# Another order of evictions, maxima and scaling between the batches of an attention block, and contiguous one-hots in the routing behind it

## The chip, the cores and the metric

The kernel runs on one core of a Trainium2 chip. Its engines work through queues of their own, each in its own order: TensorE (PE; its weight loads are shown as PEld), VectorE (DVE), ScalarE (ACT), GpSimd (POOL), and SyncE (SP), which issues most of the transfers. The metric is the device time of one execution in microseconds (us), the median of several runs.

## What is computed

An attention between tokens and states in 8 batches and 8 heads, whose output, 8 x 544 rows of 512 numbers, goes through a mixture of 8 experts:

```python
B, H, S, Ns, D = (8, 8, 512, 32, 64)
scores = scale * np.matmul(x, state.transpose(0, 1, 3, 2))
a = np.exp(scores - scores.max(-1, keepdims=True))
a /= a.sum(-1, keepdims=True) + 1e-09
xread = np.matmul(a, state)                     # tokens read states
scores2 = scale * np.matmul(state, x.transpose(0, 1, 3, 2))
a2 = np.exp(scores2 - scores2.max(-1, keepdims=True))
a2 /= a2.sum(-1, keepdims=True) + 1e-09
sread = np.matmul(a2, x)                        # states read tokens
...                                             # concat of both, heads side by side: x (8, 544, 512)
logits = x @ w_gate
local_gate = sigmoid(x @ w_local)
e = argmax(logits) if s == 0 or local_gate < 0.5 else the expert of the token before
out = softmax(logits)[e] * (np.maximum(x @ w1[e], 0.0) @ w2[e])
```

## The kernel before

The program has three stages: attention, batch by batch; routing, which decides the expert of every row and sorts the rows into blocks of 128 slots with one expert each; and the experts, block by block (38 blocks with this input). Nothing schedules the instructions: every engine takes them in the order in which the code is written.

**Attention.** `Attention.run` works on two batches at once: while `now` reads, `then`, the next batch, gets its weights. The methods of `Batch`:

- `scores` (L254, PE) forms states x tokens for all heads in two PSUM banks, `s0` and `s1`. Each has only one buffer.
- `over_tokens` takes, for each bank, the maximum over the tokens on DVE (L264, L265: `nb`) and the exponential with its sum on ACT (L268: `e2`, `z2`); DVE also writes the scores transposed in blocks of 32 into `e1` (L273).
- `over_states` takes the reciprocal of `z2` and the maximum over the states (L286, `m1`) on DVE and subtracts it on POOL (L287). `exponents` (L291, ACT) is the exponential of that, `shares` the sums and their reciprocal on DVE (L300 to L302) and the division on POOL (L303).
- `scale` (L295, ACT) multiplies `e2` by the reciprocals. `turn` (L315) transposes it on PE into the banks `t0` and `t1`, and ACT copies it out to `e` (L316). `turn_back` (L307, DVE) transposes `e1` back to `a`.
- `state_reads` multiplies `e` by the tokens on PE (L325, in bank `t0`), copies on ACT (L330, `rt`), transposes on DVE (L333, `ys`) and stores the rows through SP (L335).
- `token_reads(c)` multiplies a quarter of `a` by the states on PE (L343), in two alternating PSUM buffers `v`, and copies the result to `xr` (L346): on ACT for c = 0 and 2, on DVE for c = 1 and 3.
- `logits` multiplies `rt` by the gate's weights on PE (L352, in bank `t1`), adds up the token logits on POOL (L355), copies the states' logits to `lt` on DVE (L356), and stores `xr` (L358). The next batch's second group of transposes uses bank `t1` again.

`load_t` and `load_n` issue a batch's `x_t` (L169, two transfers) and `x_n` (L175, one) on SP, two batches ahead. `gates` fills the last columns of `sd`, which the token reads multiply by (L191 on PE, L195 on ACT). `Routing.constants` and `more_constants` write small constants (L395 to L421 on DVE); `place` (L388, ACT) holds, for every k, the number k repeated over the 40 columns.

**Routing** is mostly one chain of DVE instructions on 128 x 40 rows. `keep(n)` puts n products on PE that nobody reads (L433, bank `idle`). The chain gives every row a slot, split into block (`blk`) and place in it (`pos`). `inb` says which block a row is in, `inp` which place (both one-hot), and `slotted` (L554) multiplies them over the 40 columns, once for the rows' numbers (`who`, from `bc`) and once for their probabilities (from `pb`). `slots.row` (L576) tells POOL which rows to gather (L613); the gathered rows are transposed on DVE (L618, `xt`) for the first products of the experts (L642). Their weights `a` and `c`, 4 MB a block, come through SP (L627).

Of the kernel before, what the change touches and what calls it, by code (L numbers as in the profile page):

```python
# [10 lines left out]
BF16 = mybir.dt.bfloat16  # L11
Act = mybir.ActivationFunctionType
Alu = mybir.AluOpType
# [5 lines left out]
P = 128  # L19
B, H, S, N, DH = 8, 8, 512, 32, 64  # L20
# [4 lines left out]
SC = S // P  # L25
# [96 lines left out]
class Attention:  # L122


    def __init__(self, ctx, tc, xn, xt, st, stt, wgl, wgs, lt, rows):
# [16 lines left out]
        x_t = self.load_t(0)  # L142
        nc.sync.dma_start(out=self.sttc[1], in_=stt[:, 1:])
        nc.sync.dma_start(out=wgs.rearrange("p w k e -> p (w k e)"), in_=wgl)
        self.x = {0: (x_t, self.load_n(0))}
        self.x[1] = self.load_t(1), self.load_n(1)
# [216 lines left out]
class Routing:  # L363
# [6 lines left out]
    def constants(self, ident):  # L370
# [16 lines left out]
        place = rt.tile([P, P, COLS], BF16, name="place")  # L387
        nc.scalar.copy(place, iob.rearrange("p (k o) -> p k o", o=1).to_broadcast([P, P, COLS]))  # L388
        self.raw = pi, ci, iof, iob, identb, place

    def more_constants(self):
# [30 lines left out]
        self.consts = iof, identb, part, cols, before, ones, one, ev, down, on, turn, quarter, place  # L422

    def route(self, bank, ctx, lt, slots):
        nc, rt, ex = self.nc, self.rt, self.ex
        iof, identb, part, cols, before, ones, one, ev, down, on, turn, quarter, place = self.consts
# [3 lines left out]
        def keep(n):  # L430

            for i in range(n):
                nc.tensor.matmul(idle, lhsT=identb, rhs=place.rearrange("p k c -> p (k c)")[:, :512],  # L433
                                 start=True, stop=True)
# [84 lines left out]
        keep(28)  # L519
# [11 lines left out]
        pos = rt.tile([P, 1, COLS], BF16, name="pos")  # L531
        nc.vector.tensor_copy(pos[:, 0], pi)
# [8 lines left out]
        nc.vector.tensor_tensor(inb, place[:, :NBLK], over(blk), op=Alu.is_equal)  # L541
# [4 lines left out]
        inp = [rt.tile([P, P, COLS // 4], BF16, name=f"inp{i}") for i in range(4)]  # L546
        for i in range(4):
            cs = slice(i * COLS // 4, (i + 1) * COLS // 4)
            nc.vector.tensor_tensor(inp[i], place[:, :, cs], pos[:, :, cs].to_broadcast([P, P, COLS // 4]),
                                    op=Alu.is_equal)  # L550

        def slotted(to, x):
            for c in range(COLS):
                nc.tensor.matmul(to, lhsT=inp[c * 4 // COLS][:, :, c % (COLS // 4)], rhs=x[:, :, :, c],  # L554
                                 start=(c == 0), stop=(c == COLS - 1))
# [23 lines left out]
        def probabilities():  # L579
# [5 lines left out]
            keep(9)  # L585
# [124 lines left out]
```

## Time and profile before

| | us |
|---|---|
| median of 3 runs | 721.91 |
| the runs | 721.91, 716.51, 722.04 |
| the profiled execution | 716.16 |
| its span, first to last instruction | 714.1 |
| attention, to the last copy of `xr` | 0 to 125.5 |
| routing, to the first product of the experts | 125.5 to 169.4 |
| experts | 169.4 to 714.1 |

| engine | busy us | share of the span |
|---|---|---|
| PE | 659.9 | 92% |
| DVE | 152.1 | 21% |
| ACT | 105.7 | 15% |
| POOL | 225.9 | 32% |

In the timeline's rows the first number is the start in us from the span's start, the second how long the group of instructions took, then engine, line, operation, what it writes and reads, and, in brackets, how long the engine was idle before it and what ended that. Rows of windows give the stretch, then the busy time of PE, PEld, DVE, ACT and POOL (with the number of instructions), the granted clock of TensorE as a share of full speed, and the share and rate of the transfers.

### The profile page before, as it was taken

Reading aid. Unit: us, or ns where it says so; the run is one execution under the profiler, and the core shown is the slowest. Engines: PE = TensorE matmul, PEld = TensorE weight load, DVE = VectorE, ACT = ScalarE, POOL = GpSimd, SP = SyncE. Lnnn points to the kernel's source line nnn. Section 1 sums busy time; section 2 is a strip of 40 time slices with the busy share of each in tenths; the row PEclk is TensorE's granted clock in tenths of the full one; section 3 lists DMA queues with packets and bytes.
Section 4 is the critical chain, followed back from the end, with each engine's and each line's share of the span. In section 5 each row is a group of like instructions: output and inputs, shape, how many; then the busy total and the mean of one; then the engine's idle time right before and its main releaser. Section 6 shows DMA issues by size and latency. Waiting matters only on the chain. (4 is left out here: it accounts for less than half of the span.)

```text
span 714.1 us, 9952 instructions
## 1 busy us (share of the span) xinstructions
PE 659.9 (92%) x3958; PEld 475.6 (67%) x3958; DVE 152.1 (21%) x297; ACT 105.7 (15%) x190; POOL 225.9 (32%) x229
## 2 busy tenths in 40 slices
PE   4877778679999999999999999999999999999993
PEld 1765556257677767766776776677677767766771
DVE  6567565941010001001100100010010001000100
ACT  4545544000001100110100011001101000110010
POOL 4232332033234323422432343234224323432320
PEclk8699999867999999999999999999999999999997
DMA  9477562438899999999999999999999999999920
GB/s 293 134 253 276 189 236 66 168 143 327 301 347 338 337 334 345 329 332 357 337 323 335 344 330 332 348 341 325 330 346 338 319 344 337 327 325 352 323 74 6
DMA packets 49029, 206.03 MB, mean 289 GB/s; under 512 B 13329, under 2 KB 21649, under 8 KB 28498
## 3 DMA queue, kind: packets, MB, share of 16 engines
q1 hardware_dynamic: 40946, 186.18, 71.6%
q0 software_dynamic: 8032, 19.15, 8.9%
q8 instruction: 35, 0.57, 0.3%
q14 instruction: 16, 0.13, 0.1%
HBM read 187.47 MB, written 18.88 MB: 289 GB/s over the span
## 5 line engine op out<-in xcount | busy, mean ns | idle before, releaser
L642 PEld LDWEIGHTS ps<-xt,a 128*128 128x128 f32 x2432 | 278.2, 192 | 18.1 <-issue 18.0
L642 PE MATMUL ps<-xt,a 128*128 128x128 f32 x2432 | 278.2, 275 | 0.0
L647 PE MATMUL ps<-c,h 128*128 128x512 f32 x608 | 267.2, 592 | 0.0
L647 PEld LDWEIGHTS ps<-c,h 128*128 128x128 f32 x608 | 112.6, 190 | 127.2 <-issue 127.2
L613 POOL DMA_INDIRECT xg<-rows,row x156 | 149.6, 959 | 82.0 <-issue 47.1
L650 POOL DMA_INDIRECT out_dram<-y,tok x38 | 38.5, 1013 | 315.9 <-DVE y L649 299.0
L649 DVE TENSOR_SCALAR y<-ps,prob 128x512 f32<-128x512 f32 x38 | 28.5, 751 | 481.0 <-PE ps L647 481.0
L644 ACT ACTIVATE h<-ps 128x512 f32<-128x512 f32 x76 | 45.4, 598 | 515.2 <-PE ps L642 501.8
L343 PE MATMUL v<-sd,a 128*128 128x265 f32 x128 | 33.4, 407 | 9.5 <-ACT xr L346 9.5
L325 PEld LDWEIGHTS t<-e,x_n 128*128 128x128 f32 x256 | 32.4, 209 | 5.2 <-ACT e L316 5.2
L343 PEld LDWEIGHTS v<-sd,a 128*128 128x128 f32 x128 | 23.7, 197 | 16.3 <-ACT xr L346 12.3
L325 PE MATMUL t<-e,x_n 128*128 128x64 f32 x256 | 33.5, 294 | 0.0
L287 POOL TENSOR_TENSOR e<-e,m 128x1024 f32<-128x1024 f32 x8 | 15.3, 1912 | 49.2 <-DVE m L286 49.2
L618 DVE STREAM_TRANSPOSE xt<-xg 128x512 f32<-128x512 f32 x38 | 26.7, 702 | 6.0 <-DMA xg<-rows,row 5.4
L315 PE MATMUL t<-ident,e 128*128 128x128 f32 x64 | 11.1, 304 | 15.7 <-DVE lt L356 11.3
L303 POOL TENSOR_TENSOR e<-e,z 128x1024 f32<-128x1024 f32 x8 | 15.3, 1916 | 31.3 <-DVE lt L356 28.2
L315 PEld LDWEIGHTS t<-ident,e 128*128 128x128 f32 x64 | 7.4, 151 | 19.2 <-DVE lt L356 13.0
L254 PE MATMUL s<-x_t,sttc 64*32 64x512 f32 x128 | 12.7, 686 | 8.0 <-DMA x_t<-in_xt_dram 8.0
L554 PEld LDWEIGHTS <-inp 128*128 128x128 bf16 x80 | 11.7, 147 | 9.2 <-DVE pb L582 3.8
L433 PE MATMUL idle<-place,identb 128*128 128x512 bf16 x51 | 15.8, 474 | 0.5 <-DVE xr L346 0.5
L346 DVE COPY xr<-v 128x530 f32<-128x530 f32 x16 | 11.1, 696 | 19.1 <-PE v L343 19.1
L268 ACT ACTIVATE e<-s,nb 128x512 f32<-128x512 f32 x16 | 11.0, 687 | 24.0 <-DVE nb L265 19.0
(139 smaller groups left out, 199.2 us busy)
## 6 DMA issues: line engine op xcount, KB each, us to landing
a<-in_w_dram SPq DMA_DIRECT2D x76, 1024.0 KB, 6.8
c<-in_w_dram SPq DMA_DIRECT2D x76, 1024.0 KB
x_t<-in_xt_dram SPq DMA_DIRECT2D x16, 512.0 KB, 5.6
x_n<-in_xn_dram SPq DMA_DIRECT2D x8, 1024.0 KB, 7.5
rows<-xr SPq DMA_DIRECT2D x16, 512.0 KB, 4.2
xg<-rows,row POOLq DMA_INDIRECT x156
out_dram<-y,tok POOLq DMA_INDIRECT x38
sd<-in_st_dram SPq DMA_DIRECT2D x4, 128.0 KB, 12.7
```

Of the source, the lines that this page charges most:

```text
L287: nc.gpsimd.tensor_tensor(e1, e1, m1.to_broadcast([P, A, N]), op=Alu.subtract)
L315: nc.tensor.transpose(t[:, c * P:c * P + P], self.e2[:, u, c * P:c * P + P], at.ident)
L325: nc.tensor.matmul(rps[:, j], lhsT=self.x_n[:, c, u, k:k + 2, :].rearrange("p k d -> p (k d)"), rhs=self.e[:, c, u, 32 * k:32 * k + 64], s ...
L343: nc.tensor.matmul(v[:, u, :VW], lhsT=self.a[:, u, c * P:c * P + P], rhs=at.sd[:, b, u, :], start=True, stop=True)
L433: nc.tensor.matmul(idle, lhsT=identb, rhs=place.rearrange("p k c -> p (k c)")[:, :512], start=True, stop=True)
L613: nc.gpsimd.indirect_dma_start(out=xgs_[k % 2][:, i].rearrange("p k t -> p (k t)"), out_offset=None, in_=rows.rearrange("n q x -> (n q) x" ...
L618: nc.vector.transpose(xts_[k % 2].rearrange("p k (i t) -> p k i t", i=Q), xgs_[k % 2].rearrange("p i k t -> p k i t"))
L642: nc.tensor.matmul(hps[:, i * P:i * P + P], lhsT=a[half][:, j, i * P:i * P + P], rhs=x_t[:, j, :], start=(j == 0), stop=(j == KT - 1))
L644: nc.scalar.activation(h[:, half * 4:half * 4 + 4, :].rearrange("p m t -> p (m t)"), hps, Act.Relu)
L647: nc.tensor.matmul(yps, lhsT=h[:, m, :], rhs=c[m // 4][:, m % 4, :], start=(m == 0), stop=(m == FK - 1))
L649: nc.vector.tensor_scalar(y, yps, slots.prob[:, k:k + 1], None, Alu.mult)
L650: nc.gpsimd.indirect_dma_start(out=out, out_offset=bass.IndirectOffsetOnAxis(ap=slots.tok[:, k:k + 1], axis=0), in_=y, in_offset=None, bou ...
```

## The change

Five edits go together. The first loads bring batch 1's `x_t` ahead of batch 0's `x_n`. `more_constants` moves from the start into the first batch's reads. In the loop `over_tokens` of the next batch comes ahead of `turn_back` of this one; the copies of `xr` come ahead of `scale` and of `exponents`; and `logits` comes ahead of `shares`. `place` is cut to the 41 blocks that it is compared for. And `inp` is laid out with the 128 places side by side (five tiles of 8 columns, formerly four of 10 with the columns side by side), with 8 idle products fewer ahead of it and 9 fewer behind.

```diff
-        x_t = self.load_t(0)
+        x_t = [self.load_t(0)]
         nc.sync.dma_start(out=self.sttc[1], in_=stt[:, 1:])
         nc.sync.dma_start(out=wgs.rearrange("p w k e -> p (w k e)"), in_=wgl)
-        self.x = {0: (x_t, self.load_n(0))}
-        self.x[1] = self.load_t(1), self.load_n(1)
+        x_t.append(self.load_t(1))
+        self.x = {b: (x_t[b], self.load_n(b)) for b in range(2)}
...
         now.over_tokens()
-        route.more_constants()
+        next(gates)
         now.over_states()
-        now.exponents()
-        now.scale()
-        next(gates)
         then = Batch(self, 1)
         then.scores()
+        now.scale()
+        then.over_tokens()
+        now.exponents()
         now.shares()
         now.turn()
         for b in range(B):
             if b + 2 < B:
                 self.x[b + 2] = self.load_t(b + 2), self.load_n(b + 2)
+            if then and b:
+                then.scores()
+                then.over_tokens()
             now.turn_back()
             if then:
-                if b:
-                    then.scores()
-                then.over_tokens()
                 then.over_states()
             now.state_reads()
-            if then:
-                then.scale()
-            now.token_reads(0)
-            if then:
-                then.exponents()
-            for c in range(1, SC):
+            if b == 0:
+                route.more_constants()
+            for c in range(SC):
                 now.token_reads(c)
+                if then and c == 1:
+                    then.scale()
+                if then and c == 2:
+                    then.exponents()
+            now.logits()
             if then:
                 then.shares()
-            now.logits()
-            now = then
-            if now:
-                now.turn()
-                then = Batch(self, b + 2) if b + 2 < B else None
+                then.turn()
+            now, then = then, Batch(self, b + 2) if b + 2 < B else None
...
-        place = rt.tile([P, P, COLS], BF16, name="place")
-        nc.scalar.copy(place, iob.rearrange("p (k o) -> p k o", o=1).to_broadcast([P, P, COLS]))
+        place = rt.tile([P, NBLK, COLS], BF16, name="place")
+        nc.scalar.copy(place, iob[:, :NBLK].rearrange("p (k o) -> p k o", o=1).to_broadcast([P, NBLK, COLS]))
...
-        keep(28)
+        keep(20)
...
-        inp = [rt.tile([P, P, COLS // 4], BF16, name=f"inp{i}") for i in range(4)]
-        for i in range(4):
-            cs = slice(i * COLS // 4, (i + 1) * COLS // 4)
-            nc.vector.tensor_tensor(inp[i], place[:, :, cs], pos[:, :, cs].to_broadcast([P, P, COLS // 4]),
+        part_of = COLS // 5
+        inp = [rt.tile([P, part_of, P], BF16, name=f"inp{i}") for i in range(5)]
+        for i in range(5):
+            nc.vector.tensor_tensor(inp[i], iob.rearrange("p (o k) -> p o k", o=1).to_broadcast([P, part_of, P]),
+                                    pos[:, i * part_of:(i + 1) * part_of].to_broadcast([P, part_of, P]),
                                     op=Alu.is_equal)
...
-                nc.tensor.matmul(to, lhsT=inp[c * 4 // COLS][:, :, c % (COLS // 4)], rhs=x[:, :, :, c],
+                nc.tensor.matmul(to, lhsT=inp[c // part_of][:, c % part_of], rhs=x[:, :, :, c],
...
             slotted(prob, pb)
-            keep(9)
```

How this moves VectorE's queue shows between two batches of the loop. Here it is before, from the sums of batch 2 (`z1_476`, of `e1_413`) to the first transpose of batch 3's scores (`s0_511`, `s1_512`); the lines are numbered one higher than after the change.

```order
L300 TENSOR_REDUCE z1_476<-e1_413 128x32
L301 TENSOR_SCALAR z1_476<-z1_476 128x32
L302 RECIPROCAL z1_476<-z1_476 128x32
L356 COPY lt_69<-t1_481 32x9
L307 STREAM_TRANSPOSE a_509<-e1_413 128x1024
L264 TENSOR_REDUCE nb_524<-s0_511 128x1
L265 TENSOR_SCALAR nb_524<-nb_524 128x1
L264 TENSOR_REDUCE nb_524<-s1_512 128x1
L265 TENSOR_SCALAR nb_524<-nb_524 128x1
L273 STREAM_TRANSPOSE e1_521<-s1_512 128x512
```

The same place on VectorE after the change, where batch 2's weights are `e1_411` and batch 3's scores `s0_509` and `s1_510`:

```order
L355 COPY lt_69<-t1_476 32x9
L299 TENSOR_REDUCE z1_485<-e1_411 128x32
L300 TENSOR_SCALAR z1_485<-z1_485 128x32
L301 RECIPROCAL z1_485<-z1_485 128x32
L263 TENSOR_REDUCE nb_522<-s0_509 128x1
L264 TENSOR_SCALAR nb_522<-nb_522 128x1
L263 TENSOR_REDUCE nb_522<-s1_510 128x1
L264 TENSOR_SCALAR nb_522<-nb_522 128x1
L272 STREAM_TRANSPOSE e1_519<-s1_510 128x512
L272 STREAM_TRANSPOSE e1_519<-s0_509 128x512
L306 STREAM_TRANSPOSE a_531<-e1_411 128x1024
```

The copy of `lt` moved ahead of the sums, and `a` moved behind the maxima and transposes of the batch after.

On ScalarE the place is the reads of batch 2. Before, from batch 3's exponentials over the tokens to the copies of `e` for batch 3:

```order
L268 ACTIVATE e2_522,z2_523<-s0_511,nb_524 128x512
L268 ACTIVATE e2_522,z2_523<-s1_512,nb_524 128x512
L330 COPY rt_555<-t0_538 64x128 x2
L295 ACTIVATE e2_522<-e2_522,z2_523 128x512 x2
L346 COPY xr_564<-v_567 128x530
L291 ACTIVATE e1_521<-e1_521 128x1024
L346 COPY xr_564<-v_576 128x530
L316 COPY e_598<-t0_599 128x4x128
L316 COPY e_598<-t1_605 128x4x128
```

The same place on ScalarE after the change:

```order
L267 ACTIVATE e2_520,z2_521<-s0_509,nb_522 128x512
L267 ACTIVATE e2_520,z2_521<-s1_510,nb_522 128x512
L329 COPY rt_555<-t0_538 64x128 x2
L345 COPY xr_564<-v_565 128x530
L294 ACTIVATE e2_520<-e2_520,z2_521 128x512 x2
L345 COPY xr_564<-v_575 128x530
L290 ACTIVATE e1_519<-e1_519 128x1024
L315 COPY e_598<-t0_599 128x4x128
L315 COPY e_598<-t1_605 128x4x128
```

Both copies of `xr` moved up by one: the first ahead of the scalings, the second ahead of the exponentials.

More of the change, by code (lines that the diff above doesn't have):

```diff
@@ L421, in more_constants @@
         nc.vector.memset(ex, 0.0)
-        self.consts = iof, identb, part, cols, before, ones, one, ev, down, on, turn, quarter, place
+        self.consts = iof, iob, identb, part, cols, before, ones, one, ev, down, on, turn, quarter, place
     def route(self, bank, ctx, lt, slots):
         nc, rt, ex = self.nc, self.rt, self.ex
-        iof, identb, part, cols, before, ones, one, ev, down, on, turn, quarter, place = self.consts
+        iof, iob, identb, part, cols, before, ones, one, ev, down, on, turn, quarter, place = self.consts
         exf = ex.rearrange("p b i -> p (b i)")
@@ L530, in route @@
         nc.vector.tensor_scalar(si, si, 7, None, Alu.logical_shift_right)
-        pos = rt.tile([P, 1, COLS], BF16, name="pos")
-        nc.vector.tensor_copy(pos[:, 0], pi)
+        pos = rt.tile([P, COLS, 1], BF16, name="pos")
+        nc.vector.tensor_copy(pos[:, :, 0], pi)
         blk = rt.tile([P, 1, COLS], BF16, name="blk")
@@ L540, in route @@
         inb = rt.tile([P, NBLK, COLS], BF16, name="inb")
-        nc.vector.tensor_tensor(inb, place[:, :NBLK], over(blk), op=Alu.is_equal)
+        nc.vector.tensor_tensor(inb, place, over(blk), op=Alu.is_equal)
         bc = rt.tile([P, 2, NBLK, COLS], BF16, name="bc")
```

## The prediction, made before the changed kernel was run

> **What bounds the kernel now.** I read the page's slices first: in the last three quarters TensorE is never idle and its clock is full. The timeline of that part gives the length of one block of the experts, by the start of its first product.
>
> ```profile
> 169.45 7.87 PE L642 MATMUL ps<-xt,a 128*128 128x128 f32 x64
> ...
> 184.02 7.31 PE L642 MATMUL ps<-xt,a 128*128 128x128 f32 x64
> ...
> 198.04 7.31 PE L642 MATMUL ps<-xt,a 128*128 128x128 f32 x64
> ```
>
> Block 1 takes 198.04 - 184.02 = 14.02 us, and so do those after it; block 0 takes 14.57. The change leaves these blocks alone, so the time moves by as much as the first product of block 0, now at 169.45, moves, plus what block 0 itself gains or loses. Attention comes first. One batch of it in the timeline, token reads to token reads:
>
> ```profile
> 54.79 2.01 PE L343 MATMUL v<-sd,a 128*128 128x265 f32 x8
> ...
> 57.73 0.60 ACT L346 COPY xr<-v 128x530 f32<-128x530 f32 x1
> 58.38 2.06 PE L343 MATMUL v<-sd,a 128*128 128x265 f32 x8 [1.58 <-ACT xr L346]
> ...
> 59.41 1.06 ACT L291 ACTIVATE e<-e 128x1024 f32<-128x1024 f32 x1 [1.08 <-POOL e L287]
> ...
> 60.72 0.66 PE L315 MATMUL t<-ident,e 128*128 128x128 f32 x4
> ...
> 61.10 1.21 DVE L300 TENSOR_REDUCE z<-e 128x32 f32<-128x1024 f32 x1
> ...
> 62.28 2.17 SPq L169 DMA_DIRECT2D x_t<-in_xt_dram  x2
> ...
> 62.83 0.09 DVE L356 COPY lt<-t 32x9 f32<-32x9 f32 x1
> ...
> 62.99 0.66 PE L315 MATMUL t<-ident,e 128*128 128x128 f32 x4 [1.62 <-DVE lt L356]
> 63.06 1.92 POOL L303 TENSOR_TENSOR e<-e,z 128x1024 f32<-128x1024 f32 x1 [3.68 <-DVE lt L356]
> 63.58 1.09 PE L254 MATMUL s<-x_t,sttc 64*32 64x512 f32 x16
> ...
> 64.60 3.79 PE L325 MATMUL t<-e,x_n 128*128 128x64 f32 x32
> 65.01 1.25 DVE L307 STREAM_TRANSPOSE a<-e 128x1024 f32<-128x1024 f32 x1 [2.09 <-POOL e L303]
> 66.17 0.65 DVE L264 TENSOR_REDUCE nb<-s 128x1 f32<-128x512 f32 x1
> ...
> 67.72 1.30 DVE L273 STREAM_TRANSPOSE e<-s 128x512 f32<-128x512 f32 x2
> ...
> 68.22 2.01 PE L343 MATMUL v<-sd,a 128*128 128x265 f32 x8
> ```
>
> A batch takes 68.22 - 54.79 = 13.43 us. TensorE stands still twice. The third token read waits 1.58 us for ScalarE's copy of the first (57.73), which stands behind both scalings. The second group of transposes waits 1.62 us for the 0.09 us copy of `lt` (62.83), since its bank `t1` still holds the logits; that copy stands in VectorE's queue behind the sums (61.10) of the next batch. Both are waits for a place in a queue, not for data.
>
> **The change part by part. Loop order.** `xr` now comes ahead of the scalings and `lt` ahead of the sums, so both waits go. What is late next? In the new order VectorE turns `a` only behind the maxima and transposes of the batch after, and those wait for its scores. That closes loop A, from a token read's start to the next batch's: four token reads 4.0 (2.01 and 2.06 without the gap), logits up to the transposes 0.3 (58.38 + 2.06 to 60.72), first transposes 0.66, second ones up to the scores 0.59 (62.99 to 63.58), scores 1.09, maxima and transposes 2.85 (66.17 to 67.72 + 1.30), `a` 1.25, and 0.2 for three hand-overs: 10.9 us. Loop B is nearly as long: three token reads 3.05, ScalarE's copy 0.60, exponentials 1.06, sums and reciprocal 1.73 (61.10 to 62.83), then the same 2.85 and 1.25, hand-overs 0.3: 10.8. GpSimd's 1.92 fits beside the 2.85. TensorE's own work is 4.0 + 0.3 + 1.25 + 1.09 + 3.6 (64.60 to 68.22) = 10.2. I take **10.9 us** a batch against 13.43.
>
> ```profile
> 108.52 2.01 PE L343 MATMUL v<-sd,a 128*128 128x265 f32 x8
> ...
> 120.73 3.98 PE L343 MATMUL v<-sd,a 128*128 128x265 f32 x16
> ...
> 124.74 0.71 DVE L346 COPY xr<-v 128x530 f32<-128x530 f32 x1 [1.26 <-PE v L343]
> ```
>
> From the token reads of batch 1 to those of batch 6 (108.52) there are five such intervals: 5 x 2.53 = 12.6 us. The one to batch 7 is now 12.21. There no scores are left ahead of `a`, and loop B with the division runs: 3.05 + 0.6 + 1.06 + 1.8 + 1.92 + 1.25 + 0.4 = 10.1. That is 2.1 more. What follows to the end of the last copy (125.45) stays. The bounds per batch are 10.2, TensorE's own work, and 11.6, with 0.1 us more at each of loop A's seven steps; over six intervals that is 4 us either way.
>
> **Start.** `more_constants` no longer stands ahead of `over_states`, and batch 1's maxima and exponentials go ahead of batch 0's exponentials.
>
> ```profile
> 14.13 1.20 DVE L286 TENSOR_REDUCE m<-e 128x32 f32<-128x1024 f32 x1
> ...
> 21.65 7.09 PE L325 MATMUL t<-e,x_n 128*128 128x64 f32 x32
> 21.86 0.59 ACT L316 COPY e<-t 128x512 f32<-128x512 f32 x1 [0.27 <-PE t L315]
> ...
> 25.82 0.69 ACT L268 ACTIVATE e<-s,nb 128x512 f32<-128x512 f32 x1 [0.63 <-DVE e L273]
> ...
> 28.53 5.04 PE L343 MATMUL v<-sd,a 128*128 128x265 f32 x16
> ```
>
> Without 1.4 us of constants `m` runs from 12.7 to 13.9; then batch 1's 2.85 to 16.8, its second exponential (0.69, begun before the last transpose ends) to 17.1, batch 0's 1.06 to 18.2, two copies of 0.59 to 19.4, and the state reads begin at 19.5 instead of 21.65. They still run at half clock (TensorE is idle before them as now), so the token reads begin 2.15 us before 28.53. The constants now run behind `ys`, beside cold token reads that TensorE needs longer for. The loads of `x_t` and `x_n` that trade places are needed after 12.4 and after 19.5. The scores' banks are free only at 12.4, so the earlier `x_t` buys nothing and the later `x_n`, some 3 us on, costs nothing. ScalarE's smaller `place` ends before the maxima either way. Bounds: 0, and 5.5 if the state reads run at full clock (3.79 instead of 7.09). Attention in all: 2.15 + 12.6 + 2.1 = **16.9 us**.
>
> **Routing.** Its rows now:
>
> ```profile
> 126.44 0.49 DVE L441 TENSOR_TENSOR eq<-lt,mx 128x320 f32<-128x320 f32 x1
> ...
> 135.53 8.36 PE L433 MATMUL idle<-place,identb 128*128 128x512 bf16 x28
> ...
> 140.76 3.02 DVE L549 TENSOR_TENSOR inp<-place,pos 128x1280 bf16<-128x1280 bf16 x4
> ...
> 143.73 7.09 PE L554 MATMUL ps<-bc,inp 128*128 128x82 bf16 x40
> ...
> 146.56 0.18 DVE L566 CAST parts<-own 128x40 bf16<-128x40 f32 x1
> 150.86 0.24 DVE L570 CAST wd<-ps 128x82 bf16<-128x82 f32 x1 [4.12 <-PE ps L554]
> ...
> 152.05 0.45 DVE L576 SCALAR_TENSOR_TENSOR row<-ps,hw 128x164 int32<-128x164 f32 x1
> ...
> 155.23 10.58 PE L554 MATMUL ps<-pb,inp 128*128 128x123 bf16 x40 [3.65 <-DVE pb L582]
> ...
> 160.91 0.71 DVE L618 STREAM_TRANSPOSE xt<-xg 128x512 f32<-128x512 f32 x1 [5.38 <-DMA xg<-rows,row]
> ...
> 165.63 4.03 PE L433 MATMUL idle<-place,identb 128*128 128x512 bf16 x9
> ```
>
> The products by `inp` start at 143.73, when 28 idle products end. With 20, the eight left out are the last ones, at full clock: nine took 4.03 us at half clock, so eight take 1.8 at full, and TensorE is free some 1.7 us earlier, at 142.1. Is the first `inp` there? Each new one has 1024 elements in which `pos` repeats along the innermost axis; no row shows this for 2-byte numbers. At today's rate it takes 1024/1280 x 0.755 = 0.6 us. At the rate of L441, which repeats an operand so in 4-byte numbers (0.49 for 320, of which an estimated 0.16 is fixed), it takes 1.1 to 1.2. I take 1.1, the row of the same access: the first is ready at 142.0, one more each 1.1 us, while TensorE needs 1.4 for its eight columns. So VectorE stays ahead. It ends at 146.4 instead of 143.78, and with its own 3.0 (to 146.74 now) at 149.4; the products end at 149.3. `wd` starts at 149.6, not at 150.86: **1.2 us** (bounds 0.3 and 1.5).
>
> [...]
>
> Do contiguous `inp` weights make the 80 products faster? These rows of the clock speak against it:
>
> ```profile
> 144.00:146.00 2.00, 2.00 (x14) 1.69 (x13) 1.86 (x6) 0.00 (x0) 0.00 (x0) 1.00 0.99 418
> ...
> 148.00:150.00 2.00, 2.00 (x14) 1.69 (x13) 0.00 (x0) 0.00 (x0) 0.00 (x0) 0.50 0.09 29
> ```
>
> At clock 1.00 and at 0.50 the same 14 products stand in 2 us. The spacing is 7.09/40 = 0.177 us for 82 columns and 10.58/40 = 0.264 for 123: in proportion to the columns of `bc` and `pb`, which are read 40 elements apart as before. A load of weights that set the pace would give both the same spacing. I take no gain.
>
> Then the nine idle products go (4.03 us at half clock). Block 0 would start at 165.63 - 1.2 = 164.4 instead of 169.45, its `xt` being there at 161.62 - 1.2. But the idle products also warmed the clock. Block 0 loses 0.56 us to it now (14.57 against 14.02), so it ran at half clock for 1.1 us, up to 170.6: the clock went up 4.9 us after TensorE's dense work began at 165.63. Without the idle products block 0 itself is cold for those 4.9 us and loses 2.45. The net is 5.05 - (2.45 - 0.56) = **3.15 us**, with the 1.2 in it. If the clock stayed low for all of its 64 first products (7.3 us at full clock), the experts would get through block 0 some 1.4 us later than without the change.
>
> [...]
>
> **Sum.** 16.9 + 3.15 = 20.0 us. The profiled execution took 716.16 us (span 714.1), so 696.1. The four times shown fall into pairs, 716.16 and 716.51, 721.91 and 722.04; from the median, 721.91, it would be 701.9. I name 698, between the two, since I can't tell in which pair most runs will fall; the rivals stand on the same footing.
>
> **Rivals.** (1) The new loop is longer than its rows add up to, some 12.2 us, because a hand-over or ScalarE's queue (copy, scaling, copy, exponentials, now in one file) takes the place of the waits. Against it: ScalarE waited 1.08 us ahead of the exponentials at 59.41. Price 6 x 1.3 = 8: 706. (2) Contiguous weights do set the pace. The first 40 products are then paced by VectorE, nothing won; the second 40 end early, but block 0 waits for `xt`, 161.62 - 1.2 = 160.4 instead of 164.4: 4 us more, 694. The proportion above speaks against it. (3) Slower: `x_t`.
>
> ```profile
> x_t<-in_xt_dram SPq DMA_DIRECT2D x16, 512.0 KB, 5.6
> ```
>
> Now `a` waits for the next scores, so a late `x_t` stops everything. SyncE issues it behind the copies' writes: from the copy's end to the second half's issue 3.3 us (61.1, where the sums follow it, to 64.45), landing 5.6, half the scores 0.55, then 2.85 + 1.25 + 4.0 + 0.8 to the copy two batches on: 18.3 for two batches, 9.2 each. It decides from a landing of 9 us. At 18 us a batch costs 15.4, six cost 11.5 more than now, less 5.3 gained elsewhere: 724. For it: the same transfers in less time. Against it: today's 5.6. (4) The waits come back one for one and the start's too, at the next place in the same queues: only routing's 3 us, 715.
>
> **How the numbers follow.** Forecast 0.62, rival (1) 0.18, (2) 0.12, (4) 0.05, (3) 0.03. The range 688 to 707 takes in the forecast's bounds of 4 us, (1) and (2). A run tells 1%, 7 us, from no change: faster 0.92, same 0.05, slower 0.03.
>
> **What would show it.** Token reads 10.9 us apart at full clock; no wait of TensorE for `lt` or `xr`, but one for `a`; five `inp` of 1.1 us; products by `inp` still 0.177 and 0.264; block 0 about 20 us earlier and 16 to 17 us long. I am wrong if `a` waits for `x_t` or if GpSimd's division ends last.

## The result, and the profile after the change

| | us |
|---|---|
| median of 4 runs after (694.51 to 695.11) | 694.9 |
| median of 4 runs before (716.35 to 722.04) | 719.21 |
| ratio | 0.9661, 95% interval 0.9609 to 0.9714 |
| the profiled execution after, its span | 695.11, 693.3 |
| the profiled execution before, its span | 716.16, 714.1 |

The forecast was 698, from 688 to 707, faster. The kernel before has times near 716.4 and times near 722, and nothing here shows what parts them: against the first the change wins 3.0%, against the second 3.75%. Span against span the kernel wins 20.8 us. The timeline after the change, first the token reads (L343 is now L342):

```profile
24.96 6.23 PE L342 MATMUL v<-sd,a 128*128 128x265 f32 x16
...
37.98 4.02 PE L342 MATMUL v<-sd,a 128*128 128x265 f32 x16 [0.47 <-DVE z L282]
...
91.97 4.02 PE L342 MATMUL v<-sd,a 128*128 128x265 f32 x16 [0.44 <-DVE z L282]
101.92 4.02 PE L342 MATMUL v<-sd,a 128*128 128x265 f32 x16 [0.53 <-DVE a L306]
```

From batch 1 on, all 16 products of a batch's token reads run without a gap in 4.02 us; before, eight of them ended and the next eight waited for `xr`. The five intervals from 37.98 to 91.97 (batch 1 to batch 6) are 10.80 us each, where 13.43 stood. The wait of 0.47 us ahead of them is the one for `a`: the row names `z` (L282), which follows `a` in VectorE's queue and which the token reads don't read, and in the last row, where no `z` follows, it names `a` itself. What VectorE does in one of these intervals:

```profile
64.28 0.14 DVE L355 COPY lt<-t 32x9 f32<-32x9 f32 x1
64.36 1.20 DVE L299 TENSOR_REDUCE z<-e 128x32 f32<-128x1024 f32 x1
...
66.33 0.69 DVE L263 TENSOR_REDUCE nb<-s 128x1 f32<-128x512 f32 x1 [0.18 <-PE s L253]
...
69.14 1.20 DVE L306 STREAM_TRANSPOSE a<-e 128x1024 f32<-128x1024 f32 x1
```

From the copy of `lt` to the end of `a`, 64.28 to 70.34, VectorE stands still for one moment of 0.18 us, in which it waits for the scores: the two loops of the prediction are equally long there within these 0.18 us. The next token reads start at 70.40.

Routing and the first blocks of the experts:

```profile
116.71 7.10 PE L432 MATMUL idle<-place,identb 128*128 128x512 bf16 x20
...
121.93 5.76 DVE L548 TENSOR_TENSOR inp<-iob,pos 128x1024 bf16<-128x1024 bf16 x5
...
123.65 7.09 PE L554 MATMUL ps<-bc,inp 128*128 128x82 bf16 x40
...
130.77 0.24 DVE L570 CAST wd<-ps 128x82 bf16<-128x82 f32 x1
...
135.15 10.54 PE L554 MATMUL ps<-pb,inp 128*128 128x123 bf16 x40 [3.65 <-DVE pb L582]
...
145.50 9.42 PE L641 MATMUL ps<-xt,a 128*128 128x128 f32 x64
...
161.63 7.31 PE L641 MATMUL ps<-xt,a 128*128 128x128 f32 x64
175.64 7.31 PE L641 MATMUL ps<-xt,a 128*128 128x128 f32 x64
```

Block 0 starts 24.0 us earlier than before (145.50 against 169.45) and takes 16.13 us instead of 14.57 (its 64 first products take 9.42 us, those of a later block 7.31), so block 1 starts 22.4 us earlier (161.63 against 184.02). Later blocks take 14.01 as before. Yet the span shrank by 20.8 only, 1.6 us less than that. These 1.6 us are lost in the last block:

```profile
666.11 0.72 PE L641 MATMUL ps<-xt,a 128*128 128x128 f32 x5
668.15 6.85 PE L641 MATMUL ps<-xt,a 128*128 128x128 f32 x59 [1.32 <-issue]
```

Five products into it TensorE stands still for 1.3 us with nothing in the profile that it waits for ("issue"). The prediction had nothing of the kind; experiment 8 is about it.

### The profile page after: what moved, and what is told of

Read it like the earlier page. It is cut to its first block, busy times and chain, and to the rows that moved or that the text cites. A ratio compares the mean times of both kernels' runs of the same rounds, so it can differ in the third digit from the quotient of the medians.

```text
span 693.3 us, 9935 instructions
## 1 busy us (share of the span) xinstructions
PE 657.3 (95%) x3941; PEld 474.5 (68%) x3941; DVE 155.2 (22%) x298; ACT 102.8 (15%) x190; POOL 226.1 (33%) x229
## 5 line engine op out<-in xcount | busy, mean ns | idle before, releaser
L342 PE MATMUL v<-sd,a 128*128 128x265 f32 x128 | 34.4, 424 | 3.3 <-DVE z L282 2.8
L342 PEld LDWEIGHTS v<-sd,a 128*128 128x128 f32 x128 | 24.2, 203 | 11.2 <-DVE z L282 3.6
L253 PE MATMUL s<-x_t,sttc 64*32 64x512 f32 x128 | 11.2, 668 | 7.4 <-DMA x_t<-in_xt_dram 5.7
L554 PEld LDWEIGHTS <-inp 128*128 128x128 bf16 x80 | 10.2, 128 | 10.6 <-DVE pb L582 3.8
L554 PE MATMUL ps<-pb,inp 128*128 128x123 bf16 x40 | 10.5, 445 | 3.6 <-DVE pb L582 3.6
L267 ACT ACTIVATE e<-s,nb 128x512 f32<-128x512 f32 x16 | 11.0, 687 | 16.9 <-DVE nb L264 11.8
L263 DVE TENSOR_REDUCE nb<-s 128x1 f32<-128x512 f32 x16 | 11.0, 685 | 3.5 <-PE s L253 3.5
L345 ACT COPY xr<-v 128x530 f32<-128x530 f32 x16 | 9.6, 602 | 11.8 <-PE v L342 11.7
```

The lines of the kernel that those rows point to most:

```text
L342: nc.tensor.matmul(v[:, u, :VW], lhsT=self.a[:, u, c * P:c * P + P], rhs=at.sd[:, b, u, :], start=True, stop=True)
L345: copy(self.xr[:, c], v[:, :, :VW])
L554: nc.tensor.matmul(to, lhsT=inp[c // part_of][:, c % part_of], rhs=x[:, :, :, c], start=(c == 0), stop=(c == COLS - 1))
```

## The experiments

Every experiment is a kernel of its own. The table has their times; the kernel before, run beside them on the same chips, had medians of 715.9 to 716.8. The change, the three edits of the loop and the rebuilt routing ran four times, the others once. The third column is the distance from one batch's token reads to the next one's.

| kernel | time | token reads, full clock | first product of block 1 |
|---|---|---|---|
| before | 716.2 | 13.43 apart | 184.02 |
| copies of `xr` alone | 723.7 | 12.84 | |
| `logits` alone | 721.8 | 13.48 | |
| `over_tokens` alone | 726.2 | 13.07 | |
| `logits` and `over_tokens` | 701.5 | 11.08 | |
| the three of the loop | 699.45 | 10.80 | 166.86 |
| all (the change) | 694.9 | 10.80 | 161.63 |
| all, idle products back | 697.0 | 10.81 | 165.03 |
| all, `inp` as before | 692.5 | 10.81 | 160.09 |
| all, `bc` and `pb` contiguous | 689.85 | 10.79 | 157.77 |
| routing rebuilt | 686.55 | 10.80 | 154.21 |

### 1 to 4. Which of the loop's edits opens it?

Four kernels on the base of the kernel before. The first has the copies of `xr` ahead of scalings and exponents:

```diff
-            now.token_reads(0)
-            if then:
-                then.exponents()
-            for c in range(1, SC):
+            for c in range(SC):
                 now.token_reads(c)
+                if then and c == 1:
+                    then.scale()
+                if then and c == 2:
+                    then.exponents()
...
```

> The kernel before with one edit: the copies of xr ahead of the scalings and of the exponentials. Theory of waits (a wait that goes is worth its length): TensorE loses its 1.58 us before the third token read, so a batch takes 13.43 - 1.58 = 11.85 us. Theory of loops: behind the waits stands a loop of VectorE, GpSimd and ScalarE that no copy of xr is in: maximum over the states 1.2, subtraction 1.9, exponentials 1.1, sums and reciprocal 1.7, division 1.9, a 1.2, the next batch's maxima and transposes 2.85, reciprocal of z 0.3, with eight hand-overs 0.6: 12.7 to 12.9 us. So a batch takes 12.8 us, and the whole kernel is 4 us faster.

The second has `logits` ahead of `shares` and nothing else:

```diff
+            now.logits()
             if then:
                 then.shares()
-            now.logits()
```

> The kernel before with one edit: logits (and with it the copy of lt) ahead of shares. Theory of waits: the 1.62 us before the second group of transposes go, 11.8 us a batch. Theory of loops: the loop of maxima, subtraction, exponentials, sums, division, a and the next maxima stays, and the sums now wait for the last token read and the logits behind it as well: 13.4 to 13.6 us a batch, nothing won.

The third has the next batch's maxima ahead of `a` and nothing else:

```diff
-            now.turn_back()
             if then:
                 if b:
                     then.scores()
                 then.over_tokens()
+            now.turn_back()
+            if then:
                 then.over_states()
```

> The kernel before with one edit: the next batch's maxima, exponentials and transposes ahead of a. Theory of waits: neither wait of TensorE is touched, so 13.4 us, or more since a comes 2.85 us later. Theory of loops: the loop of VectorE and GpSimd is opened, but now a waits for scores, which stand behind the transposes that wait for lt, which stands behind the sums: token reads 2.0 with the copy of xr behind the scalings, exponentials, sums, lt, transposes, scores, maxima, a: 12.9 us a batch.

The fourth has the second and third edit together:

> The kernel before with two edits: logits ahead of shares, and the next batch's maxima ahead of a; xr stays behind the scalings. Theory of waits: 1.62 us go, at best 11.8 us. Theory of loops: both loops are open, what is left is token reads, logits, transposes, scores, maxima, a, plus 0.3 us for the third token read, which waits for the late copy of xr: 11.2 us a batch, though each of the two edits alone wins 0.5 us or nothing.

Measured in the timeline while the clock stands at 1.00: 12.84, 13.48, 13.07 and 11.08 us a batch, each within 0.2 us of what was expected from the loops, while the sums that subtract waits gave 11.85, 11.8, 13.4 or more, and 11.8 at best. The view of waits says why. Its columns are who waits for whom, the total, the number of times and the longest, all between 36 and 62 us. The kernel before:

```profile
PE t L315 <- DVE lt L356: 3.2, 2, 1.6
PE v L343 <- ACT xr L346: 3.2, 2, 1.6
```

With the copies of `xr` alone, and with `logits` alone:

```profile
PE t L314 <- DVE lt L355: 6.0, 3, 2.1
```

```profile
PE v L343 <- ACT xr L346: 6.6, 2, 3.3
```

With the copies first, the wait for `xr` is gone and the one for `lt` grew from 1.6 to 2.1 us, so that of 1.58 us only 0.59 are won. With `logits` first, the wait for `lt` is gone and the one for `xr` doubled to 3.3, so nothing is won at all. The two waits were two places at which TensorE stood against the same loop, the one that runs through VectorE's queue (maxima over the states, GpSimd's subtraction, ScalarE's exponentials, sums, GpSimd's division, `a`, the next maxima); whichever place is cleared, the loop stays nearly as long, and TensorE waits longer at the other. With `over_tokens` first this loop is open, but `a` now waits for scores, which stand behind the transposes that wait for `lt`: that wait stays at 1.6, the one for `xr` shrinks to 0.5 at most, and the batch is 0.4 us shorter. With `logits` and `over_tokens` together both loops are cut open: 11.08 us, and what is left are short waits for `a` (again under the name of `z`) and for `xr`.

```profile
PE v L344 <- DVE z L284: 0.9, 2, 0.5
PE v L344 <- ACT xr L347: 0.5, 2, 0.2
```

The copies of `xr` then remove the last wait for ScalarE, 0.24 us: 10.80.

That all three single edits were slower than the kernel before, by 6 to 10 us, was not expected: at full clock their batches are no longer than before within 0.05 us, and for the copies alone a gain of 4 us had been forecast. Windows of the kernel with `logits` alone show where the time goes (the last but two number of a row is the granted clock):

```profile
88.00:90.00 2.00, 2.00 (x6) 1.58 (x5) 0.00 (x0) 1.59 (x2) 0.29 (x1) 0.50 0.16 25
90.00:92.00 2.00, 2.00 (x13) 1.19 (x13) 0.77 (x3) 0.07 (x1) 0.00 (x0) 0.50 0.00 0
```

The clock falls to 0.50 inside the loop: in this kernel in four stretches of 3.4 or 6.8 us. In the other two the stretches within the loop are of 3.4 or 13.6 us (and one of 10.2 in the last batch, with the copies alone), and one of the third kernel's catches a whole batch:

```profile
78.12 1.96 PE L255 MATMUL s<-x_t,sttc 64*32 64x512 f32 x16
80.01 7.09 PE L326 MATMUL t<-e,x_n 128*128 128x64 f32 x32
86.89 6.25 PE L344 MATMUL v<-sd,a 128*128 128x265 f32 x16
```

Scores of 1.96 instead of 1.09 and state reads of 7.09 instead of 3.79 us make that batch 16.3 us long (70.62 to 86.89, the token reads before it to these). In the kernel with `logits` and `over_tokens`, and after the change, the clock stays at 1.00 through the loop, as it does in both profiles of the kernel before. What tips it was not settled: each of the three kernels ran once, and the times of the kernel before differ by as much (716.35 to 722.04), so it isn't shown that these edits cost the clock.

### 5. The loop alone, without the start and without routing

All three edits of the loop on the kernel before.

> The kernel before with the three reorderings of the loop alone (copies of xr ahead of scalings and exponents, logits ahead of shares, the next batch's over_tokens ahead of turn_back); start and routing as before. My theory: both waits go, token reads 10.8 to 10.9 us apart instead of 13.43, the clock stays full in the loop, token reads of batch 0 still at about 28.5, block 0 about 15.5 us earlier than before (at 154.0) and 14.6 long: 700.7 us against a before of 716.2. Rival (the shorter batch needs the earlier start or the earlier loads of x_t too): batches above 12 us and over 707 us.

Median 699.45 us (699.0 to 700.67), ratio 0.9742, interval 0.9685 to 0.9799.

```profile
28.16 5.17 PE L343 MATMUL v<-sd,a 128*128 128x265 f32 x16
40.12 4.02 PE L343 MATMUL v<-sd,a 128*128 128x265 f32 x16 [0.47 <-DVE z L283]
50.92 4.02 PE L343 MATMUL v<-sd,a 128*128 128x265 f32 x16 [0.47 <-DVE z L283]
...
152.28 7.88 PE L642 MATMUL ps<-xt,a 128*128 128x128 f32 x64
```

Batches of 10.80 us, so they need neither the earlier start nor the earlier loads. The loop is worth 17.2 us at block 0 (152.28 against 169.45), 1.7 more than expected. Of the 17.2, 1.2 are won up to the second token reads (40.12 against 41.35, and 41.31 in the kernel before of experiment 10), a stretch which the sum had left out; 15.4 come from there to the last token reads and 0.5 in routing. Against this kernel, the change's second token reads come 2.14 us earlier (37.98 against 40.12). That is what the change's other edits of attention's stage, those of the start and the smaller `place`, are worth together.

### 6. The idle products, and the layout of `inp`

The changed kernel with `keep(28)` ahead of the products by `inp` and `keep(9)` behind the second ones again:

> The changed kernel with both groups of idle products as before (28 ahead of the products by inp, 9 behind the second ones). My theory: wd 1.7 us later, nine idle products of 4.0 us ahead of block 0, which then takes 14.6 instead of 16.1 us; the first product of block 1 comes 4.2 us later than in the changed kernel (165.8 against 161.6), time 699 us, or 698 if the 1.3 us stall in the last block goes away. Rival (the idle products paid for themselves through the clock): block 1 at the same time, 695 us.

```profile
124.79 5.53 PE L554 MATMUL ps<-bc,inp 128*128 128x82 bf16 x31
...
150.47 7.85 PE L642 MATMUL ps<-xt,a 128*128 128x128 f32 x64
165.03 7.31 PE L642 MATMUL ps<-xt,a 128*128 128x128 f32 x64
```

Block 1 is 3.4 us later than in the changed kernel (165.03 against 161.63, the last token reads at 101.89 and 101.92): the idle products hold nearly all of routing's gain of 3.6 us, and the rival, that they paid for themselves through the clock, falls. The clock did gain by them: block 0 runs at 0.50 for 1.1 us of its 14.56 here, for 3.8 of its 16.13 in the changed kernel. The products by `inp` start 1.14 us later (124.79 against 123.65), not 1.7: they follow the idle ones in both kernels, and eight more of those took only that long. The time, 697.0, is 2 us better than the 699 expected and 1 us better than the 698 named for a last block without the stall, which is what this one is.

The changed kernel with `inp` laid out as before, columns side by side, still in five tiles, and for that with `place` at its full size again:

```diff
-        inp = [rt.tile([P, part_of, P], BF16, name=f"inp{i}") for i in range(5)]
+        inp = [rt.tile([P, P, part_of], BF16, name=f"inp{i}") for i in range(5)]
...
-                nc.tensor.matmul(to, lhsT=inp[c // part_of][:, c % part_of], rhs=x[:, :, :, c],
+                nc.tensor.matmul(to, lhsT=inp[c // part_of][:, :, c % part_of], rhs=x[:, :, :, c],
...
```

> The changed kernel with inp laid out as before (columns side by side, so TensorE loads weights at a stride), still in five tiles with the new numbers of idle products. My theory: spacing is set by the columns of bc and pb, so the products stay at 0.177 and 0.264 us; each inp takes 0.6 instead of 1.15 us, which nobody waits for; block 0 within 0.3 us of the changed kernel's 145.5, time 695 us. Rival (contiguous weights are what the routing's gain comes from): products slower than 0.177 and 0.264, block 0 over 1 us later.

```profile
121.64 3.09 DVE L549 TENSOR_TENSOR inp<-place,pos 128x1024 bf16<-128x1024 bf16 x5
122.69 7.09 PE L554 MATMUL ps<-bc,inp 128*128 128x82 bf16 x40
...
134.19 10.59 PE L554 MATMUL ps<-pb,inp 128*128 128x123 bf16 x40 [3.65 <-DVE pb L582]
```

The products take 7.09 and 10.59 us, as with contiguous weights, and each `inp` takes 0.62 instead of 1.15: contiguous places bring TensorE nothing. Block 0 came 0.9 us earlier (144.59), where 0.3 was expected. 0.3 of that is there at the last token reads (101.64 against 101.92), and the rest is again in the idle products ahead: the 20 of them took 6.44 us here (116.41 to 122.85) against 7.10, since the clock was back at 1.00 sooner (about 120.4 against 122.0). The windows of this kernel and of the changed one:

```profile
120.00:122.00 2.00, 2.00 (x10) 0.84 (x8) 1.97 (x4) 0.00 (x0) 0.00 (x0) 0.90 0.97 406
```

```profile
120.00:122.00 2.00, 2.00 (x6) 0.76 (x5) 1.97 (x4) 0.00 (x0) 0.00 (x0) 0.50 1.00 422
```

The same program differs by some tenths from one execution to the next (block 0 of the changed kernel took 16.13 us and, in experiment 8, 15.83); whether contiguous places cost so little or nothing stays open. The time is 692.5 where 695 was expected: block 1 comes 1.5 us earlier than in the changed kernel (160.09 against 161.63), and the last block has no stall.

### 7. What sets the products' spacing

The changed kernel with `bc` and `pb` laid out so that the columns which TensorE streams lie side by side (`blk` and `inb`, from which they are made, follow):

```diff
-        bc = rt.tile([P, 2, NBLK, COLS], BF16, name="bc")
+        bc = rt.tile([P, COLS, 2, NBLK], BF16, name="bc")
...
-            pb = rt.tile([P, 3, NBLK, COLS], BF16, name="pb")
+            pb = rt.tile([P, COLS, 3, NBLK], BF16, name="pb")
...
```

> The changed kernel with bc and pb laid out so that the 82 or 123 columns that TensorE streams lie side by side (instead of 40 elements apart); inb, bc and pb then repeat an operand along the innermost axis and take 1.8 instead of 1.0 us for 1640 elements. My theory (the stride of the streamed operand sets the spacing): the second products fall from 0.264 to 0.13 or less, 10.5 to about 5.3 us; the first ones are paced by VectorE's inp (0.144 each) instead of 0.177; VectorE's own chain then ends last and makes wd 1.4 us later; block 0 about 1 us earlier, 694 us. Rival (loading weights or the product itself sets the spacing): 0.177 and 0.264 stay, block 0 about 3 us later, 698 us.

```profile
123.16 5.76 DVE L549 TENSOR_TENSOR inp<-iob,pos 128x1024 bf16<-128x1024 bf16 x5
124.44 0.48 PE L555 MATMUL ps<-bc,inp 128*128 128x82 bf16 x8 [1.85 <-DVE inp L549]
...
131.78 0.23 DVE L571 CAST wd<-ps 128x82 bf16<-128x82 f32 x1
...
138.70 4.32 PE L555 MATMUL ps<-pb,inp 128*128 128x123 bf16 x40 [6.20 <-DVE pb L583]
```

Forty products of `pb` take 4.32 us instead of 10.54, both at a clock of 0.50, and eight of `bc` take 0.48, which is 0.06 each instead of 0.177. The stride of the streamed operand set the spacing, as the proportion to the columns and its indifference to the clock had said. In the two traces that is 0.264/123 = 2.1 ns a column with the columns 80 bytes apart, 0.108/123 = 0.9 side by side; why the stride costs that much was not shown. VectorE's side came as expected too: it is now the first products' pace, and its own chain makes `wd` 1.0 us later (131.78 against 130.77; 1.4 were expected). Time 689.85, better than the 694 expected: 1.6 us are the stall that is missing in the last block, and block 0 was 14.32 us long against 16.13, with the clock at 1.00 from 143.9 on, 0.5 us into the block, and not from 3.8 us into it.

### 8. The stall in the last block

The changed kernel once more, and then with 13 instead of 9 idle products at the start of routing, where TensorE waits in any case:

> The changed kernel once more. Its profile showed TensorE standing still for about 1.4 us five products into the last block, which took 15.7 instead of 14.1 us; none of the kernels tried so far showed that. Theory A (it belongs to this program): the last block takes 15.7 us again, 695 us. Theory B (a chance of that execution): 14.1 us, 693.3 us.

> The changed kernel with 13 instead of 9 idle products at the start of routing, where TensorE waits anyway: eight more instructions ahead of the experts. Theory A1 (the stall in the last block comes from where a jump's target lies in TensorE's instructions): it goes away or sits in another place, 693.4 us when it goes. Theory A2 (it comes from the order of the transfers or from what the last block does): 15.7 us for the last block again, 695 us.

The last blocks of the two, in this order:

```profile
665.65 0.72 PE L641 MATMUL ps<-xt,a 128*128 128x128 f32 x5
666.68 6.85 PE L641 MATMUL ps<-xt,a 128*128 128x128 f32 x59 [0.32 <-issue]
```

```profile
665.41 0.27 PE L641 MATMUL ps<-xt,a 128*128 128x128 f32 x1
666.14 7.30 PE L641 MATMUL ps<-xt,a 128*128 128x128 f32 x63 [0.46 <-issue]
```

The same program stalls at the same place, behind the fifth product, but for 0.3 us instead of 1.3 (time 693.62), between the two theories. With four products more ahead, each with its load of weights, the stall moves four products forward, behind the first, and lasts 0.46 us (time 694.03). So in these three profiles it sits at a fixed place in TensorE's instructions, and its length differs from one execution to the next (1.32 and 0.32 us with the same program); that a jump's target lies there, as theory A1 has it, was not shown. Of the other last blocks only that of experiment 7 has longer first products (7.51 us against 7.31). The transfers of the changed kernel's profiled execution have a queue of the kind "instruction", q8, with 36 packets of 16 KB: about one every 21 us through the experts, and four within 11 us around the start of the last block. One of these ends at 666.67, and TensorE's next product starts at 668.15, 1.5 us later. But the kernel before has such packets there too, one of them up to 689.39, and its last block, from 688.50 on, has no stall (7.31 us). What the packets hold and what TensorE stood still for was not shown.

### 9. Routing rebuilt on these findings

`bc` and `pb` contiguous for TensorE; the column numbers repeated ahead by GpSimd and the places by ScalarE, so that VectorE compares packed operands; VectorE's own chain (L559 to L568) behind `row`; `pb` in five pieces; 10 idle products fewer.

```diff
+        for i in range(5):
+            cs = slice(i * part_of, (i + 1) * part_of)
+            nc.scalar.copy(posb[:, cs], pos[:, cs].to_broadcast([P, part_of, P]))
...
+            for i in range(5):
+                cs = slice(i * part_of, (i + 1) * part_of)
+                for d in range(3):
+                    nc.vector.tensor_tensor(pb[i][:, d], inb[:, cs], ...
```

> The changed kernel with bc and pb laid out for TensorE's streaming (columns side by side), the column numbers laid out ahead by GpSimd, the places repeated by ScalarE so that VectorE compares packed operands (inp 0.6 us instead of 1.15), VectorE's own chain moved behind row, pb in five pieces, 10 idle products fewer. My theory: products 0.06 to 0.11 us apart; wd at 126.7 instead of 130.8; own chain 3.0 and five pieces of pb of 1.2 us follow row, xt comes 9.1 us after row; block 0 at 138.3 instead of 145.5, some 17 us long at the lower clock; block 1 6 to 7 us earlier than in the changed kernel, 687 us. Rival (block 0 then waits for the weights a or the gathers): block 0 not before 142, 690 us.

```profile
122.75 3.09 DVE L551 TENSOR_TENSOR inp<-iob,posb 128x1024 bf16<-128x1024 bf16 x5
123.50 3.14 PE L557 MATMUL ps<-bc,inp 128*128 128x82 bf16 x40 [2.44 <-DVE inp L551]
126.67 0.24 DVE L563 CAST wd<-ps 128x82 bf16<-128x82 f32 x1 [0.82 <-PE ps L557]
...
131.25 6.30 DVE L588 TENSOR_TENSOR pb<-inb,parts 128x328 bf16<-128x328 bf16 x15
...
137.97 0.71 DVE L624 STREAM_TRANSPOSE xt<-xg 128x512 f32<-128x512 f32 x1
...
138.94 8.57 PE L648 MATMUL ps<-xt,a 128*128 128x128 f32 x64 [0.34 <-DVE prob L598]
...
154.21 7.31 PE L648 MATMUL ps<-xt,a 128*128 128x128 f32 x64
```

Median 686.55 us (686.07 to 687.27), ratio to the kernel before 0.9572, interval 0.953 to 0.9614. `wd` stands where it was expected, block 0 starts 6.6 us earlier than in the changed kernel, block 1 7.4. Block 0 now starts 0.3 us behind the end of `xt` (138.68) and of the last products by `pb` (138.60); its row names `prob`, the copy behind `xt` in VectorE's queue. `xt` starts with no wait ahead of it, straight behind VectorE's own work, the pieces of `pb` from 131.25 on and two short instructions. It comes 9.7 us behind the end of `row` (128.31), where in the changed kernel it came 8.4 us behind it, after a wait for the gathered rows. So it is VectorE's queue that bounds routing's end now, and not the gathers.

### 10. The kernel before, once more

> The kernel before once more, for its clock in the loop. Its times fall into a group at 716.5 and one at 722; the listed mean clocks are 0.961 to 0.973 in the first and 0.952 to 0.954 in the second. Theory: in the second group the clock falls inside the attention loop, so if this run takes 722, stretches between 40 and 125 us stand at 0.50 and the batches there are longer than 13.43; if it takes 716.5, the loop is at 1.00 throughout. Rival: the loop is the same in both, and the 5.5 us are lost elsewhere.

It took 716.35 us, with the loop at 13.43 us a batch and the clock at 1.00 in it. So no execution of 722 us was caught, and neither the theory nor its rival was tried.

## Why the prediction held, and where its terms were off

The forecast was 20.0 us less than the profiled 716.16; the profiled execution after the change took 21.05 less. 698 was named, between the 696.1 and the 701.9 that the sum gave; the change took 694.9.

- **What bounds it** held. Experts' blocks are unchanged, and the time moves with the first products of blocks 0 and 1.
- **The loop, 10.9 us a batch**: 10.80. The waits were those for a place in a queue, and the two new loops are equally long within the 0.18 us that VectorE waits for scores. Experiments 1 to 4 show that it was right to sum up loops and not to subtract waits: with `logits` first one wait of 1.6 us is gone and nothing won.
- **Five intervals, 12.6 us**: 13.2. The last one, 2.1: 2.26.
- **The first interval** is the term that the sum left out: the loop's edits alone bring the second token reads 1.2 us earlier (experiment 5), though the clock is at 0.50 in the first 2.4 us of that stretch (up to 30.6 us).
- **The start, 2.15 us**: the number is right, the path to it isn't. The state reads began 3.57 us earlier, not 2.15 (21.65 before):

```profile
18.08 7.09 PE L324 MATMUL t<-e,x_n 128*128 128x64 f32 x32 [2.80 <-ACT e L315]
```

  They need only the first of the two copies of `e`, as they did before the change (it ends at 21.60 there); the working waited for both, which is 0.6 us. `m` began 0.4 us earlier than it was put. And the earlier `x_t` does buy something: batch 1's scores end at 13.37 instead of 15.55, and the maxima that moved up run at 13.45 and 14.24. How much of it comes from which edit wasn't tried. But 1.1 us were lost again, since the clock rose only 0.8 us earlier, at 29.9 after the change (first row) against 30.7 before (second row):

```profile
28.00:30.00 2.00, 2.00 (x6) 1.50 (x6) 0.71 (x1) 0.91 (x2) 0.00 (x0) 0.53 0.17 25
30.00:32.00 2.00, 2.00 (x9) 1.60 (x8) 0.36 (x1) 1.98 (x4) 0.10 (x1) 0.83 0.10 16
```

  So the first token reads took 6.23 us, against 5.17 with the loop's edits alone, and from 3.20 us at their start (24.96 against 28.16) 2.14 were left at the second ones. That this meets 2.15 is luck. It holds some tenths of chance as well: with the other kernels of the changed code the second token reads come between 37.50 and 38.08. Together attention's end moved 18.8 us (the end of the last copy of `xr` from 125.45 to 106.69), where 16.9 was forecast. The state reads at 7.09 us stayed slow, as taken; the bound of 5.5 wasn't reached.
- **`wd` 1.2 us earlier** counted from attention's end: 1.33 (130.77 - 106.69 against 150.86 - 125.45). Each `inp` of 1024 elements takes 1.15 us, the rate of the row that repeats an operand, and 0.62 in experiment 6, where no operand repeats along the innermost axis. The 0.16 us that the working took as fixed in that row was the author's estimate; VectorE's 128x1 rows (L265 before) take 0.15. The reason given for the start of the products, the end of the idle ones, is right as well.
- **No faster products**: 0.177 and 0.264, unchanged. Rival (2) falls, and experiment 7 shows the positive side of the argument.
- **Block 0 cold, 16 to 17 us**: 16.13. The clock came back about 3.8 us after 145.50, where 4.9 were taken:

```profile
148.00:150.00 2.00, 2.00 (x14) 2.00 (x13) 0.00 (x0) 0.00 (x0) 0.95 (x1) 0.67 1.00 406
```

  With 0.67 on average over these 2 us it rose at 149.3. The net of routing is 3.6 us instead of 3.15 (58.57 from attention's end to block 1 before, 54.94 after). Of it 3.4 are the idle products.
- **Rival (1)**, 12.2 us a batch, falls: ScalarE's file of copies, scalings and exponents doesn't end last. **Rival (3)** falls: `x_t` lands in 5.7 us (5.6 before), and TensorE waits for it nowhere in the loop. **Rival (4)**, waits that come back elsewhere one for one, is wrong for the whole change and right for `logits` alone; of the wait that the copies of `xr` remove, two thirds come back.
- **Not foreseen**: the stall in the last block, which took 1.6 us of the gain away again.

So the result came out 3.1 us better than named. 1.9 of that is the choice of 698 above the sum's 696.1. The rest is attention, 1.9 us better than summed (1.2 up to the second token reads, 0.6 in the five intervals, 0.2 in the last), and routing, 0.5 us better, with 1.6 us of stall against them; what remains, 0.4 us, lies outside the span or between executions.

## What to carry to other kernels

When an engine stands still at two places in a period, ask whether one loop runs through both before adding up the waits: here either edit alone moved its wait, in part or whole, to the other place (1.6 us became 2.1 or 3.3), and only edits that together cut open the loops through VectorE's queue brought 2.4 to 2.6 us a batch. When products come at a spacing that keeps in proportion to their columns and doesn't change with the clock, look at the stride of the streamed operand and not at the weights: `bc` and `pb` side by side gave 0.06 for 0.177 and 0.108 for 0.264. And idle products that keep the clock up have to be set against what waits behind them: here, taking them away left block 0 at 0.50 for 3.8 us instead of 1.1, which cost 1.6 us, and won 5.0 at its start.

## What the runs showed of the hardware that was not expected

- The granted clock fell to 0.50 in the middle of the loop in the three kernels with one edit, in which TensorE never waited longer than 3.3 us from 36 us on, and cost up to 3.2 us a batch there (16.27 against 13.07); with batches of 10.8 to 11.1 us it stayed at 1.00 in all eight profiles that list it. The stretches at 0.50 within the loop lasted 3.4, 6.8 or 13.6 us, one in the last batch 10.2.
- Reading columns 80 bytes apart cost TensorE about 2.15 ns a column in the products by `inp` (0.177 us for 82, 0.264 for 123), with the same 14 products in 2 us at a clock of 1.00 and of 0.50.
- In the last block of the changed kernel TensorE stood still behind the fifth product, for 1.32 us in one execution and 0.32 in another; with eight instructions more ahead it did so behind the first, for 0.46 us. The block's 64 first products took 8.9, 7.9 and 8.0 us instead of 7.31.
- In five profiles (experiments 1, 2, 6 with `inp` as before, 7 and 10) the clock is listed at 1.00 from 20 to 30 us, though the state reads of batch 0 take the same 7.09 us there as in the profiles before and after the change, which list 0.50.
